# Attention with an MLP behind it: the first chunk's softmax sums in 64x32 tiles, and one load moved to another queue

## The chip, the cores and the metric

One core of a Trainium2 chip runs the whole program. The time is device microseconds (us) from start to end of one execution; the kernel before took 416.88 us (median of 3 runs, 416.04 to 417.06). The profile is of one more execution, whose span is 417.9 us. The engines are TensorE (PE in the profile; its weight loads are PEld), VectorE (DVE), ScalarE (ACT), GpSimd (POOL), and SyncE (SP), which only issues transfers.

## The reference, cut to what matters

```python
q, k, v: (8 batches, 12 heads, 448 positions, 64)      # float32
q_n, k_n = q / rms(q) * g_q, k / rms(k) * g_k           # rms over the 64
scores = q_n @ k_n.T / 8
attn = exp(scores - max) / (sum(exp(scores - max)) + 1e-9)
x = (attn @ v), heads side by side                       # (3584, 768)
h = x @ w_in                                             # (3584, 2048)
g = h + sin(alpha * h) ** 2 / alpha
out = g @ w_out                                          # (3584, 768)
```

The kernel takes exp without subtracting the maximum, since normalised queries and keys keep the scores small. What matters here is the denominator: for each head and each query the sum of exp over 448 keys, and then the product of `attn @ v` with its reciprocal.

## The kernel before, in words

**Chunks.** The 12 heads of a batch are worked on in three chunks of four heads. In a chunk, a head has an index `pp` (which half of the 128 SBUF partitions its keys lie on) and an index `hi` (which half of a tile's columns). Chunk number `ci` is 3 times the batch plus 0, 1 or 2. `load_qk(ci)` fetches q and k of a chunk, `load_v(b, c)` fetches v. The first two chunks of the program have been special: the loads of their k were issued by ScalarE (`load_qk(0, nc.scalar)`, `load_qk(1, nc.scalar)`), all others by SyncE.

**Plans.** The order of work on every engine is written out by hand. The strings `STAGE_0` (batch 0), `STAGE_1` (batch 1) and `STAGE_N` (batches 2 to 7) list tokens, and every engine executes its instructions strictly in the order in which the tokens issue them:

- `q`, `u`, `r`, `g`, `k`, `t` with a chunk: square (GpSimd, L283), reduce (VectorE, L292), reciprocal root (ScalarE, L301 and L302), fold in the gains (GpSimd, L288), scale (GpSimd, L311), transpose by a transfer that SyncE issues (L321). A second digit is q (0) or k (1). Chunks 3 to 5 in a plan are those of the next batch.
- `S`: one score tile, four matmuls of 64x64 with 448 columns (L358), and its exp on ScalarE (L361).
- `o`, `v`: for the batch's first chunk, the matmuls that sum exp over the keys with a matrix of ones ("ones 0") and those with v ("values 0"), seven key tiles each (L406). `x`, `y`, `z`: the same for the second and third chunks together, in tiles of 64x32 already. A digit says how many key tiles.
- `f` or a number: steps of the second product of the batch before, used as filler between score tiles: eight matmuls of 64x64 with 384 columns each (L528).
- `V`, `l`: loads of v (issued by GpSimd) and of q and k (issued by SyncE).

After the plan comes `first_product` (96 matmuls of 128x128 with 448 columns, L449, with the sine on ScalarE at L427), beside which the tokens of a second table run at the given step (`h_plan`). So a stage is: 56 filler steps, 21 score tiles, `o`, `v`, `x`, `y`, `z`, then the first product. After the last batch the second product runs alone (L509).

**PSUM.** There are four pairs of banks. The digit string of a stage says which pair each new PSUM tile takes; it has to have been given back by its last user.

**The step that is touched.** `attend(b, "ones 0")`: for each of seven key tiles, four matmuls of 64x64, one for each (`hi`, `pp`); the weights are ones, the moving side is exp with 448 queries, and the output strip `o` is 64 partitions, so that the same sum stands on all 64 partitions on which the head's 64 output features will stand. Then ScalarE takes Ln and Exp(-x) of the whole [128, 2, 448] tile (L412, L413), which is the reciprocal `rec`, and VectorE multiplies the values by it (L421).

Of the kernel before, what the change touches and what calls it, by code (L numbers as in the profile page):

```python
# [17 lines left out]
try:  # L18
# [8 lines left out]
ACT = mybir.ActivationFunctionType  # L27
# [22 lines left out]
)  # L50
STAGE_N = (
    (
# [3 lines left out]
    ),  # L56
    "01232302102020301301320321310130210231023",
    {-1: 'l6 u51 V12', 1: 'k41', 2: 't4 l7', 3: 'g5'},
)
LAST = "0123012"  # L60

# [7 lines left out]
def kernel(  # L69
# [23 lines left out]
    nc = tc.nc  # L93
    B, H, S, D = q.shape
# [8 lines left out]
    NJ = S // REST  # L103
    assert P == 2 * REST == 2 * D
    NC = NP // 2
# [28 lines left out]
    def bank_pair(name, dtype=F32):  # L134
        slot = int(upcoming.popleft())
        free_at.remove(slot)
        ps = psum.tile([P, 2, 2048 // mybir.dt.size(dtype)], dtype, tag=f"ps{slot}", name=name)
        slot_of[id(ps)] = slot
        return ps

    def give_back(ps):
        free_at.append(slot_of.pop(id(ps)))
# [3 lines left out]
    def strip(c, pp, hi):  # L146

        s = 2 * hi + (pp if c == 1 else 1 - pp)
        return slice(s * 32, s * 32 + 32)

    def load_qk(ci, k_queue=nc.sync):

        b, dp = ci // NC, ci % NC
        qk[ci] = inp.tile([P, 2, 2 * NJ, D], F32, tag="qk", name="qk")
        for which, src, queue in ((0, q, nc.sync), (1, k, k_queue)):
            heads = src[b].rearrange("(dp hi pp) (p j) d -> dp pp p hi (j d)", hi=2, pp=2, j=NJ)[dp]
            rows = qk[ci][:, which].rearrange("p (hi j) d -> p hi (j d)", hi=2)
            if ci == 0:
                continue
            if dp < 2:  # L160
                queue.dma_start(out=rows, in_=heads.rearrange("pp p hi x -> (pp p) hi x"))
            else:
                for pp in range(2):
                    queue.dma_start(out=rows[pp * 64:pp * 64 + 64], in_=heads[1 - pp])
        if ci == 0:
            for hi in range(2):
                for which, src, queue in ((0, q, nc.sync), (1, k, k_queue)):
                    heads = src[b].rearrange("(dp hi pp) (p j) d -> dp hi pp p (j d)", hi=2, pp=2, j=NJ)[dp, hi]
                    rows = qk[ci][:, which].rearrange("p (hi j) d -> p hi (j d)", hi=2)
                    queue.dma_start(out=rows[:, hi], in_=heads.rearrange("pp p x -> (pp p) x"))  # L170
                if hi == 0:
                    load_g()
# [17 lines left out]
    def load_g():  # L190
        for i, (src, queue) in enumerate(((g_q, nc.sync), (g_k, nc.scalar))):
            queue.dma_start(out=g_rows[:, i], in_=src.rearrange("(a d) -> a d", a=1))

    load_qk(0, nc.scalar)
    load_qk(1, nc.scalar)
    load_qk(2)
    nc.gpsimd.dma_start(out=small, in_=moe_alpha.rearrange("(mt p) -> mt p", p=P))
    nc.scalar.preload_act_table_set(EXP_LN)
# [2 lines left out]
    ones = const.tile([P, D], BF16)  # L201
# [58 lines left out]
    qkT, expT, xT = {}, {}, {}  # L260
# [125 lines left out]
    def attend(b, what, tiles=range(NJ)):  # L386

        kind, both = what.split()  # L390
        both = both == "1"
        if tiles[0] == 0:
            avs[what] = bank_pair("av")
        av = avs[what]
        pre = presums.get(b) if what == "ones 0" else None
        last = 1 if pre else NJ - 1
        for j in tiles:
            for hi in range(2):
                for c in ((1, 2) if both else (0,)):
                    for pp in range(2):  # L400
                        r = slice(pp * 64, pp * 64 + 64)
                        o, k = (strip(c, pp, hi), c - 1) if both else (slice(hi * 64, hi * 64 + 64), pp)
                        d = slice(kind == "high", D, 2) if both and kind != "ones" else slice(D // 2 if both else D)
                        w = ones[r, d] if kind == "ones" else vb[b][r, 2 * c + hi, j, d]
                        x = pre.parts[j] if pre else expT[b * NC + c, j]
                        nc.tensor.matmul(av[o, k, :S], w, x[r, hi, :], start=(j == 0), stop=(j == last))  # L406
        if tiles[-1] < last:
            return
        if kind == "ones":
            rec = recs[both] = pre.t if pre else rpool.tile([P, 2, S], F32, tag="rec", name="rec")  # L410
            for k in ((0, 1), (1, 2)) if both and b == 0 else ((0, 2),):
                nc.scalar.activation(rec[:, slice(*k)], av[:, slice(*k), :S], ACT.Ln)  # L412
                nc.scalar.activation(rec[:, slice(*k)], rec[:, slice(*k)], ACT.Exp, scale=-1.0)  # L413
            give_back(avs.pop(what))
        else:
            if b not in xT:
                xT[b] = xpool.tile([P, KT, S], BF16, tag="xT", name="xT")
            first = 0 if not both else 2 if kind == "low" else 3
            for k in (slice(0, 1), slice(1, 2)) if both and b == 0 else (slice(0, 2),):
                kts = slice(first + k.start * (1 + both), first + (k.stop - 1) * (1 + both) + 1, 1 + both)  # L420
                nc.vector.tensor_mul(xT[b][:, kts, :], av[:, k, :S], recs[both][:, k])  # L421
            give_back(avs.pop(what))
# [185 lines left out]
    for b in range(B):  # L608
        plan, slots, h_plan = (STAGE_0, STAGE_1, STAGE_N)[min(b, 2)]
        if b:  # L610
            nc.scalar.preload_act_table_set(EXP_LN)
            fillers.extendleft(reversed(second_product(b - 1)))
        tiles = deque((b * NC + c, j) for c in range(NC) for j in range(NJ))
        upcoming.extend(slots)
        done = {what: 0 for what in STEPS}
        for x in tokens_of(plan):
            if x in "Ff":
                fill(x == "f")
            elif x[0] == "S":
                scores(*tiles.popleft(), int(x[1:] or 0))  # L620
            elif x[0] in STEPS:
                n = int(x[1:] or 1)
                attend(b, STEPS[x[0]], range(done[x[0]], done[x[0]] + n))
                done[x[0]] += n
            else:
                step(b, x)
        first_product(b, {i: [lambda t=t: step(b, t) for t in tasks.split()] for i, tasks in h_plan.items()})
        assert not upcoming and not tiles
# [32 lines left out]
```

## Time and profile before

| what | value |
|---|---|
| time, median of 3 | 416.88 us |
| span of the profile | 417.9 us |
| busy: PE, ACT, POOL, DVE | 95%, 76%, 68%, 54% |
| granted TensorE clock | full speed (0.998) |
| first product of batch 0 waits for its last weights until | 41.79 us |
| from one first product's start to the next, batches 2 to 7 | 47.3 us |
| last first product ends, second product alone begins | about 393 us |
| transfers | 54.5 MB, 130 GB/s over the span |

A stage's time is read from the start of one block of L449 matmuls to the next. The busy share of PE over the span is held down by the first 42 us (loads and the first batch's normalisation) and by a few waits in the stage of batch 1; how full the later stages are is shown further down. Every row's count and mean duration come from the groups of instructions, and the spacing of matmuls from the timeline of PE.

### The profile page before, as it was taken

What the parts mean: (1) busy time and instruction counts of PE and PEld (TensorE: products, weight loads), DVE (VectorE), ACT (ScalarE), POOL (GpSimd) and SP (SyncE); (2) the same over time, 40 slices, a digit from 0 to 9 for tenths busy, and PEclk for the clock granted to TensorE, in tenths of its full rate; (3) what the DMA queues carried; (4) which work ended last, traced back from release to release, by engine and by line L of the source; (5) the groups of instructions that cost most, each with busy time, mean ns of one, the idle gap of its engine ahead of it and who ended that gap; (6) DMA issues with size and microseconds to landing.
All of it is one profiled execution on the core that took longest, in us unless ns stands there. A gap on an engine that the chain in (4) does not pass through costs nothing.

```text
span 417.9 us, 14897 instructions
## 1 busy us (share of the span) xinstructions
PE 397.1 (95%) x6598; PEld 238.2 (57%) x6601; DVE 227.1 (54%) x339; ACT 317.4 (76%) x467; POOL 285.3 (68%) x270
## 2 busy tenths in 40 slices
PE   2797999889999999999999999999999999999996
PEld 2243558645666557655666456655576556665563
DVE  5786475426674565564575466655565464335511
ACT  4897789748889679877889688987889688886600
POOL 4999889966786879597796688597795784003300
PEclk9999999999999999999999999999999999999999
DMA  8999999798085744847374744736385521620022
GB/s 244 212 220 255 167 218 156 168 284 105 3 164 131 168 139 83 175 92 156 101 175 119 174 134 80 176 81 164 104 131 158 93 46 27 96 61 0 2 75 75
DMA packets 66788, 54.51 MB, mean 130 GB/s; under 512 B 38164, under 2 KB 62500, under 8 KB 66724
## 3 DMA queue, kind: packets, MB, share of 16 engines
q1 hardware_dynamic: 53250, 40.06, 37.8%
q0 software_dynamic: 12512, 11.81, 19.7%
q10 hardware_dynamic: 962, 1.70, 1.1%
q8 instruction: 51, 0.84, 0.8%
q14 instruction: 13, 0.11, 0.1%
HBM read 45.62 MB, written 11.01 MB: 136 GB/s over the span
## 4 chain that ended last, share of the span: by engine, by line
PE 86%; DMA 6%; POOL 4%; issue 2%; DVE 1%; ACTq 0%; SPq 0%; ACT 0%; DVEq 0%; POOLq 0%
PE hps L449 34%; PE ops L528 29%; PE av L406 11%; PE sc L358 6%; PE ops L509 5%; DMA w_in<-in_moe_w_in_dram 3%; DMA qk<-in_k_dram 2%; POOL sq L283 1%; DMA out_dram<-osb 1%; POOL qk L288 1%; POOL vb L182 0%; POOL vb L185 0%; SPq L499 0%; POOL w_in L244 0%; DVE osb L534 0%
## 5 line engine op out<-in xcount | busy, mean ns | idle before, releaser
L361 ACT ACTIVATE expT<-sc 128x896 bf16<-128x896 f32 x168 | 144.9, 914 | 16.9 <-PE sc L358 16.0
L449 PE MATMUL hps<-xT,w_in 128*128 128x448 bf16 x768 | 146.8, 353 | 2.1 <-DMA w_in<-in_moe_w_in_dram 2.1
L528 PE MATMUL ops<-w_out_sb,g_sb 64*64 64x384 bf16 x3072 | 145.6, 323 | 0.2 <-ACT expT L361 0.2
L435 DVE SCALAR_TENSOR_TENSOR g_sb<-s,inv_alpha_sb,hps 128x448 bf16<-128x448 f32 x128 | 80.8, 677 | 67.3 <-POOL s L430 66.9
L449 PEld LDWEIGHTS <-w_in 128*128 128x128 bf16 x768 | 74.4, 98 | 74.0 <-issue 3.0
L528 PEld LDWEIGHTS <-g_sb 64*64 64x64 bf16 x3072 | 91.3, 107 | 38.0 <-issue 2.7
L430 POOL TENSOR_TENSOR s<-s 128x448 f32<-128x448 f32 x64 | 59.5, 932 | 74.7 <-ACT s L427 50.2
L427 ACT ACTIVATE s<-hps,alpha_sb 128x448 f32<-128x448 f32 x128 | 74.4, 626 | 43.2 <-PE hps L449 40.4
L283 POOL TENSOR_TENSOR sq<-qk 128x896 f32<-128x896 f32 x44 | 73.3, 1682 | 26.1 <-DMA qk<-in_k_dram 21.1
L311 POOL TENSOR_TENSOR qkn<-qk,inv 128x448 bf16<-128x448 f32 x80 | 72.7, 938 | 2.5 <-ACT inv L302 2.0
L358 PE MATMUL sc<-qkT 64*64 64x448 bf16 x672 | 58.3, 356 | 3.6 <-DVE qkT L343 2.1
L534 DVE COPY osb<-ops 128x384 f32<-128x384 f32 x48 | 26.7, 557 | 51.3 <-PE ops L528 46.1
L288 POOL TENSOR_TENSOR qk<-qk,gg 128x896 f32<-128x896 f32 (+1 forms) x25 | 50.3, 2016 | 1.2 <-ACT g_sb L280 1.1
L292 DVE TENSOR_REDUCE ms<-sq 128x14 f32<-128x896 f32 x44 | 46.7, 1078 | 6.4 <-POOL sq L283 6.3
L421 DVE TENSOR_TENSOR xT<-av,rec 128x896 bf16<-128x896 f32 (+1 forms) x26 | 25.6, 1015 | 37.2 <-ACT rec L413 30.7
L406 PE MATMUL av<-expT,vb 64*32 64x448 bf16 (+1 forms) x1120 | 37.9, 350 | 2.7 <-issue 2.0
L432 ACT ACTIVATE s<-s 128x448 f32<-128x448 f32 x64 | 36.9, 577 | 3.0 <-DVE g_sb L435 0.2
L358 PEld LDWEIGHTS <-qkT 64*64 64x64 bf16 x672 | 20.7, 107 | 17.3 <-issue 7.9
L406 PEld LDWEIGHTS <-vb 64*32 64x32 bf16 (+1 forms) x1120 | 19.5, 95 | 16.7 <-issue 6.8
L535 DVE TENSOR_TENSOR osb<-osb,ops 128x384 f32<-128x384 f32 x48 | 26.6, 554 | 1.7
L406 PE MATMUL av<-expT,ones 64*32 64x448 bf16 (+1 forms) x672 | 24.5, 349 | 0.0
L509 PE MATMUL ops<-w_out_sb,g_sb 128*128 128x384 bf16 x128 | 21.0, 326 | 0.0
(46 smaller groups left out, 173.5 us busy)
## 6 DMA issues: line engine op xcount, KB each, us to landing
out_dram<-osb SPq DMA_DIRECT2D x39, 192.0 KB, 3.7
qk<-in_q_dram SPq DMA_DIRECT2D x15, 448.0 KB, 5.5
qk<-in_k_dram SPq DMA_DIRECT2D x14, 448.0 KB, 6.3
qk<-in_q_dram SPq DMA_DIRECT2D x18, 224.0 KB, 4.3
qk<-in_k_dram SPq DMA_DIRECT2D x16, 224.0 KB, 4.7
vb<-in_v_dram POOLq DMA_DIRECT2D x16, 224.0 KB, 4.4
w_out_sb<-in_moe_w_out_dram POOLq DMA_DIRECT2D x4, 768.0 KB, 7.7
out_dram<-osb SPq DMA_DIRECT2D x26, 96.0 KB, 3.4
```

The source lines that it names most:

```text
L283: nc.gpsimd.tensor_mul(st.sq[w], qk[ci][:, w], qk[ci][:, w])
L288: nc.gpsimd.tensor_mul(x, x, gg.to_broadcast([P, len(heads) * NJ, D]))
L292: nc.vector.reduce_sum(st.ms[:, w, rows], st.sq[w][:, rows], axis=AX.X)
L311: eng.tensor_mul(n[:, :, hi, :], x[:, hi], inv[:, hi].unsqueeze(2).to_broadcast([P, NJ, D]))
L358: nc.tensor.matmul(sc[pp * 64:pp * 64 + 64, hi, :S], qkt[r, 1, j * REST:(j + 1) * REST], qkt[r, 0, :], start=True, stop=True)
L361: nc.scalar.activation(expT[c, j], sc[:, :, :S], ACT.Exp, scale=SCALE)
L406: nc.tensor.matmul(av[o, k, :S], w, x[r, hi, :], start=(j == 0), stop=(j == last))
L427: nc.scalar.activation(s1, hps, ACT.Sin, scale=alpha_sb[:, m, :])
L430: nc.gpsimd.tensor_mul(s2, s1, s1)
L435: nc.vector.scalar_tensor_tensor(g_sb[:, m, (b % 2) * S:(b % 2 + 1) * S], s2, inv_alpha_sb[:, m, :], hps, op0=ALU.mult, op1=ALU.add)
L449: nc.tensor.matmul(ps[:, m % 2, :S], w_in_sb[m * 2 // MT][:, kt, m % (MT // 2) * P:(m % (MT // 2) + 1) * P], x[:, kt, :], start=(kt == ORD ...
L528: nc.tensor.matmul(st["ps"][os, r, :HALF], g_sb[rs, m, c0 + o * 64:c0 + o * 64 + 64], w_out_sb[rs, m, half * HALF:(half + 1) * HALF], star ...
```

## The change

The sums of the first chunk, for all batches but the first, no longer use four 64x64 tiles but eight of 64x32: the 448 queries are split in two halves (`qh`), and each half's sum goes to its own strip of 32 partitions. This uses 32 columns of ones where 64 held the same value, and each matmul streams 224 columns where it streamed 448; there are twice as many. A head's 64 partitions then hold, in their two strips of 32, two different halves of the queries, both in columns 0 to 223. ScalarE takes Ln of that half width, writes Exp(-x) once to columns 224 to 447 and once in place, and four transfers from SBUF to SBUF, issued by SyncE, bring each strip's reciprocals to the partner strip. After that `rec` is as it was.

The plan of batches 2 to 7 is replaced: `o7` stands earlier, among score tiles and fillers, and `v` follows in three pieces after seven more score tiles. The order of GpSimd's work, of the loads and of the PSUM pairs changes with it. `STAGE_1` stays as it is. The loads of k for the second chunk of the program go to SyncE's queue.

```diff
 STAGE_N = (
     (
-        "1 r2 q31 q30 f 2 S V10 f 3 V11 f f k20 2 S 3 S 2 k21 S u31 q40 1 t2 1 g3 1 S 1 f u30 S 2 f S f S "
-        "r3 q41 f f 1 l5 1 f S 4 u40 S S 5 S S u41 o7 v7 S S 5 S 2 q51 f S 2 S q50 k31 k30 2 S g4 1 u50 S "
-        "2 r4 t3 1 S z3 x7 k40 y7 z1 z2 z1 "
+        "q40 f V11 5 f 1 f S f 1 S g4 2 f r2 f S u40 1 f S 1 f S 2 S k21 2 S k20 t2 q30 2 f 1 S q31 f f 1 "
+        "l5 f S o7 1 u30 2 q41 V12 u31 1 S 2 S 2 S 3 r3 1 u41 S 1 V10 g3 1 q51 S S 3 S v2 v4 S v1 k30 2 S "
+        "1 S 1 S 3 S k31 r4 1 x7 y7 t3 z7 q50 "
     ),
-    "01232302102020301301320321310130210231023",
-    {-1: 'l6 u51 V12', 1: 'k41', 2: 't4 l7', 3: 'g5'},
+    "01232313130132332302312310213212301230123",
+    {-1: 'k40', 0: 'g5 u51 l6', 2: 'k41 t4', 8: 'u50 l7'},
 )
-    load_qk(1, nc.scalar)
+    load_qk(1)
+        halved = what == "ones 0" and b > 0
         for j in tiles:
+            if halved:
+                for hi in range(2):
+                    for qh in range(2):
+                        for pp in range(2):
+                            r, o = slice(pp * 64, pp * 64 + 64), slice((2 * hi + qh) * 32, (2 * hi + qh) * 32 + 32)
+                            nc.tensor.matmul(av[o, pp, :S // 2], ones[r, :D // 2], expT[b * NC, j][r, hi, qh * S // 2:(qh + 1) * S // 2],
+                                             start=(j == 0), stop=(j == NJ - 1))
+                continue
...
+            if halved:
+                cols = [slice(0, S // 2), slice(S // 2, S)]
+                nc.scalar.activation(rec[:, :, cols[0]], av[:, :, cols[0]], ACT.Ln)
+                nc.scalar.activation(rec[:, :, cols[1]], rec[:, :, cols[0]], ACT.Exp, scale=-1.0)
+                nc.scalar.activation(rec[:, :, cols[0]], rec[:, :, cols[0]], ACT.Exp, scale=-1.0)
+                for hi in range(2):
+                    for qh in range(2):
+                        src, dst = (slice((2 * hi + x) * 32, (2 * hi + x) * 32 + 32) for x in (qh, 1 - qh))
+                        nc.sync.dma_start(out=rec[dst, :, cols[qh]], in_=rec[src, :, cols[qh]])
```

More of the change, by code (lines that the diff above doesn't have):

```diff
@@ L410, in attend @@
             rec = recs[both] = pre.t if pre else rpool.tile([P, 2, S], F32, tag="rec", name="rec")
-            for k in ((0, 1), (1, 2)) if both and b == 0 else ((0, 2),):
+            if halved:
[7 more added lines that the diff above has]
+                        nc.sync.dma_start(out=rec[dst, :, cols[qh]], in_=rec[src, :, cols[qh]])
+            for k in () if halved else ((0, 1), (1, 2)) if both and b == 0 else ((0, 2),):
                 nc.scalar.activation(rec[:, slice(*k)], av[:, slice(*k), :S], ACT.Ln)
```

## The prediction, made before the changed kernel was run

> **What bounds the kernel now.** I read three views in this order. First the chain of waits that ended last, to see which engine carries the time:
>
> ```profile
> PE 86%; DMA 6%; POOL 4%; issue 2%; DVE 1%; ACTq 0%; SPq 0%; ACT 0%; DVEq 0%; POOLq 0%
> PE hps L449 34%; PE ops L528 29%; PE av L406 11%; PE sc L358 6%; PE ops L509 5%; DMA w_in<-in_moe_w_in_dram 3%; DMA qk<-in_k_dram 2%; POOL sq L283 1%; DMA out_dram<-osb 1%; POOL qk L288 1%; POOL vb L182 0%; POOL vb L185 0%; SPq L499 0%; POOL w_in L244 0%; DVE osb L534 0%
> ```
>
> TensorE's own work is the chain, and av L406, which holds the edited matmuls, has 11% of it. Second, busy times by stretches, cut at the starts of the first products, to see whether a stage has any idle PE time to lose or to win:
>
> ```profile
> 90.20:137.50 47.30, 47.30 (x853) 28.82 (x854) 27.76 (x41) 37.97 (x57) 32.16 (x28) 1.00 0.58 115
> 137.50:184.80 47.30, 47.30 (x855) 28.82 (x854) 27.08 (x40) 39.06 (x58) 37.34 (x34) 1.00 0.58 136
> 280.00:327.30 47.30, 47.25 (x855) 28.83 (x852) 27.09 (x40) 39.05 (x58) 37.07 (x34) 1.00 0.58 134
> ```
>
> The columns are length, then PE, PEld, DVE, ACT and POOL busy, then clock, DMA share and GB/s. PE is busy for 47.30 of 47.30 us: these stages are as long as TensorE's work, so each us of PE work that goes is a us of time, until ACT (39) or POOL (37) becomes the bound. Third, PE's timeline in one stage, for the spacing of the matmuls:
>
> ```profile
> 218.49 1.49 PE L406 MATMUL av<-expT,ones 64*64 64x448 bf16 x28
> 219.82 1.49 PE L406 MATMUL av<-expT,vb 64*64 64x448 bf16 x28
> ...
> 227.67 0.36 PE L358 MATMUL sc<-qkT 64*64 64x448 bf16 x4
> 227.96 0.76 PE L406 MATMUL av<-expT,vb 64*32 64x448 bf16 x24
> 228.53 1.51 PE L406 MATMUL av<-expT,ones 64*32 64x448 bf16 x56
> 229.86 1.89 PE L406 MATMUL av<-expT,vb 64*32 64x448 bf16 x72
> ```
>
> The first column is the start. The 28 edited matmuls take 219.82 - 218.49 = 1.33 us to the next group's start: seven waves of four tiles, 0.19 each. At 64x32, 56 matmuls take 229.86 - 228.53 = 1.33 us: seven waves of eight, also 0.19. The tiles run side by side and the columns streamed set the time. From the last 64x64 wave to the first 64x32 wave it is 0.29 where a wave is 0.19: a change of tile shape costs 0.10.
>
> [...] The trace is already at 1.33/56 = 23.8 ns with tiles side by side, [...] but nothing in it shows a lasting rate faster than that, and the change asks for 12 ns. [...] The smallest stores in the trace, 96 KB, land 3.4 us after issue on SyncE and 2.4 on ScalarE[...].
>
> **The matmuls, batches 2 to 7.** Length against columns: L449 (448 columns) runs 96 matmuls in 18.27 us of the chain, 0.190 each; L509 (384 columns) 128 in 20.82, 0.163 each. That is 0.027 for 64 columns, so 224 columns fewer make a wave of 0.190 - 3.5 x 0.027 = 0.096. Seven waves of eight tiles: 0.67 us. Removed: 1.33. Gross gain 0.66 a stage.
>
> The new plan puts `o7` between a score tile and a filler step, both 64x64; before it stood among 64x64 work and needed no change of shape. So two are added. Entering costs 0.10. Leaving is in the stage of batch 1:
>
> ```profile
> 83.13 0.38 PE L406 MATMUL av<-expT,vb 64*32 64x448 bf16 x8 [0.43 <-DVE osb L535]
> 83.45 0.38 PE L358 MATMUL sc<-qkT 64*64 64x448 bf16 x4
> 83.76 0.38 PE L406 MATMUL av<-expT,vb 64*32 64x448 bf16 x8
> ```
>
> 0.32 and 0.31 between starts, so 0.13 for leaving. Together 0.23; net 0.66 - 0.23 = 0.43 a stage. `v`, now in three pieces, is 64x64 among 64x64 work, and `x y z` enters and leaves its shape once as before. Six stages: **2.6 us**.
>
> **The same in batch 1.** There the old plan gives `o2` and `o5` apart: four changes of shape, 0.66 - 0.46 = 0.20. I count it as nothing. Behind it PE waits for a chain that its matmuls don't set: SyncE issues two transposes from 71.66 to 75.09 as soon as GpSimd has scaled chunk 2, then six stores, whose landing at 81.81 frees the output buffer that VectorE needs at 81.93. The four new transfers come after the fourth of those stores, so the two tiles waited for are not delayed, but chunk 5's loads and the later stores are, by four issues of about 0.6 = 2.4 us. GpSimd's square of chunk 5 then ends near 89.5 in place of 87 and its work up to the snake near 93.5; the first sine comes 4.4 us into the first product (237.0 against 232.6 in a later stage), here at 94.6. Hidden, by 1 us.
>
> **ScalarE.** Ln and Exp of 896 columns go (0.92 + 0.95); Ln at 448 (0.53) and two Exps at 448 (0.58 each) come: 1.69 for 1.87. ACT is busy 39 of 47, so this is worth nothing.
>
> **The four transfers.** Each moves 32 x 2 x 224 x 4 bytes = 57 KB. Issue: 0.36 to 0.70 us on SyncE's rows; I take 0.6, so 2.4 us a stage on an engine that issues for some 18 of 47 us (six transposes at 1.33, eight loads at 0.65, eight stores at 0.6). Landing: 2.4 to 4.3 us (the smallest store, a 224 KB load); I take 3. Dating the new plan on PE's clock, with 0.325 for a filler step and 0.19 for a score tile: `o7` runs at 11.8 to 12.7 us of the stage, ScalarE is done by about 14.5, SyncE has issued `t2` and `l5` by about 15.2, the transfers by 17.6, and they land at 20.6 (20.0 to 21.9). The multiplication by `rec` follows `v1`, which ends at 21.1 by the same count. So they are just hidden; VectorE may sit up to 0.8 us on them. Behind it on VectorE wait the copies of output tiles out of PSUM, and for those PE. With four bank pairs and ScalarE's exps ahead of the score tiles I expect such a wait to be absorbed.
>
> **The rest of the new plan.** GpSimd starts a stage with `q40`, which needs `l7`, issued late in the stage before. `k41` ends some 2 us later than before, so `l7` is issued at about 247 where it was 244.8 in the stage of 203 to 251; q of it landed 3.6 to 3.8 us after issue in those windows, thus at 251. GpSimd's last snake square ends 1.8 us into the new stage, later than that: no wait. From there q 1.64, V 0.74, g 2.07 and `k21 k20` 3.62 end at 9.9 us; `t2` lands by 14.6. Chunk 2's first score tile, the 15th, comes at 18.2: 3.6 us of slack. The sums per engine are those of before.
>
> **The head.** The k of the second chunk is issued by SyncE behind its q: at about 2.5 in place of 2.16. GpSimd's gate waits for that k until 10.44 now, ScalarE's squares until 10.40. On one queue q and k of chunk 1 come ahead of chunk 2's loads, which SyncE issues from 4.40, so the k may land earlier by up to 2 us. But the chain goes on to the weights at 41.79, with the DMA engines 80 to 90% busy in every slice up to there: an earlier gate mostly reorders the same bytes. At most the 2.1 us that the first product waits for w_in; I take 0.3.
>
> **Sum.** 416.88 - 2.6 - 0.3 = 414.0.
>
> **Rivals.** (a) Rate of instructions: [...] 419 in all. For it: [...] a rate never seen here. Against: waves at 23.8 ns already, and PEld is busy only 28.8 of 47.3. Chance 0.12. (b) SyncE's queue: transfers late, VectorE held, then PE. If they land 2 us later than I say, or the stores behind them do, a stage loses 0.3 to 1.3 of what it won: 415.5 to 421, middle 418. For it: only 0.5 us of slack[...]. Against: SyncE idle more than half the stage. Chance 0.16. (c) The head does move by 1 to 2 us: 412.5. For it: the chain passes through that k. Against: busy DMA. Chance 0.14. The forecast: 0.58, spread 413.4 to 414.8.
>
> **How the numbers follow.** Faster (below 415.6): 0.58 + 0.14 + 0.02 of (b) = 0.74. Same: 0.08, from (b). Slower: 0.12 + 0.06 = 0.18. The range runs from 412.2, within (c), to 418.4, within (b), and leaves out (a), the worse half of (b) and the lower part of (c), about 0.2.
>
> **What would show it.** In the timeline after, the 56 matmuls of the sums should span 0.67 us plus 0.23 of edges, stages should measure 46.87, and PE should have no idle time in them. [...] PE idle released by VectorE, with VectorE released by a transfer of `rec`, proves (b). A first product of batch 0 that resumes well before 41.8 proves (c). Stages of 47.3 or more would make the forecast wrong.

## The result, and the profile after

The changed kernel takes 439.91 us (median; 438.48 to 442.74), the kernel before 416.46 in the same session: ratio 1.0575, interval 1.0517 to 1.0633. It is slower by 5.7%. The forecast was 414.0, and the time lies far above the range too. Below, medians take all runs of a kernel, and ratios leave out runs that are more than 1.5% above its fastest.

The chain of waits that ended last, of the kernel after:

```profile
PE 73%; DMA 14%; ACT 5%; SPq 3%; DVE 3%; issue 1%; DVEq 0%; POOL 0%; POOLq 0%
PE hps L467 33%; PE ops L546 21%; PE av L415 8%; DMA rec<-rec 7%; PE ops L527 5%; PE sc L358 4%; DMA qk<-in_k_dram 4%; ACT expT L361 3%; SPq L428 2%; DMA w_in<-in_moe_w_in_dram 2%; DVE xT L439 2%; PE av L404 1%; DVE ms L292 1%; SPq L517 1%; ACT rec L423 1%
```

TensorE had 86% of it before, now 73%. A row that did not exist is fourth: the landing of the new transfers, 7% of 441 us, with their issue on SyncE (L428) at 2% and VectorE's multiplication (L439) at 2%. So the path that sets the end leaves TensorE, and it leaves it for the transfers.

Busy times by stretches, of the kernel after, cut at the starts of the first products (columns as in the prediction):

```profile
196.21:247.28 51.07, 48.73 (x881) 29.28 (x882) 27.11 (x40) 39.09 (x59) 36.84 (x33) 0.97 0.59 130
350.79:397.69 46.90, 46.90 (x881) 28.63 (x882) 22.95 (x36) 37.95 (x55) 14.80 (x15) 1.00 0.26 66
```

Two things are to be seen. The last stage, that of batch 7, is 46.90 us long and full: the forecast for every stage was 46.87. This batch has no next one, so no q, k or v is loaded while its transfers run. The other five are 51.1 to 52.0 us long, have 2.3 to 3.3 us of idle PE time (51.07 - 48.73 = 2.34 in the one shown), and their clock is 0.97 where it was 1.00. What they have and the last has not is loads.

PE's timeline of the kernel after, in the stage that starts at 196.21:

```profile
226.01 0.36 PE L358 MATMUL sc<-qkT 64*64 64x448 bf16 x4
226.30 0.86 PE L404 MATMUL av<-expT,ones 64*32 64x224 bf16 x56
227.10 1.49 PE L546 MATMUL ops<-w_out_sb,g_sb 64*64 64x384 bf16 x32
...
236.84 0.50 PE L546 MATMUL ops<-w_out_sb,g_sb 64*64 64x384 bf16 x8
239.68 0.38 PE L358 MATMUL sc<-qkT 64*64 64x448 bf16 x4 [2.35 <-DVE xT L439]
```

The 56 sums take 227.10 - 226.30 = 0.80 us with the edge behind them, and their entry 0.29 where a wave is 0.19: what the prediction worked out (0.67, and edges of 0.10 and 0.13). Ten microseconds later PE stands for 2.35 us, released by VectorE's multiplication. VectorE's and SyncE's timelines of the kernel after, of the same stage:

```profile
238.54 1.09 DVE L439 TENSOR_TENSOR xT<-av,rec 128x896 bf16<-128x896 f32 x1 [3.38 <-DMA rec<-rec]
```

```profile
224.51 3.41 SPq L321 DMA_TRANSPOSE qkT<-qkn  x2
227.97 1.40 SPq L164 DMA_DIRECT2D qk<-in_q_dram  x2
229.41 1.26 SPq L164 DMA_DIRECT2D qk<-in_k_dram  x2
230.77 3.01 SPq L428 DMA_DIRECT2D rec<-rec  x4
```

SyncE issues two transposes, then chunk 5's loads (`l5`, four of 224 KB), and only then the four transfers; VectorE starts on what they bring at 238.54. The last `v` matmul ends at about 235.7, so VectorE is about 2.9 us late, and the pair of banks that `v` holds goes back that much later. At 239.68 a score tile needs that pair. ScalarE had `rec` ready early: its last Exp starts at 228.42.

PE's idle time is not the whole loss. Busy times of the kernel after, in three stretches of 3.41 us around the wait:

```profile
237.27:240.69 3.42, 1.07 (x29) 0.87 (x28) 1.09 (x1) 1.58 (x3) 3.42 (x4) 1.00 0.46 160
240.69:244.10 3.41, 3.41 (x71) 1.61 (x68) 1.11 (x2) 1.69 (x4) 3.41 (x4) 0.50 0.02 5
244.10:247.51 3.41, 3.41 (x138) 1.76 (x123) 0.87 (x1) 2.75 (x3) 1.47 (x2) 1.00 0.52 126
```

The sixth number after the length, counts in brackets left out, is the granted clock: 1.00, then 0.50 for 3.41 us, then 1.00 again. At 0.50 TensorE was half as fast: in the window from 42.71 to 46.13, also at 0.50, the matmuls of L467 started 0.373 us apart, behind it 0.189. So 3.41 us at half speed cost 1.71. Idle 2.35 plus 1.71 is 4.06, of the 51.07 - 46.90 = 4.17 that this stage loses.

The clock records of the twelve traces say more. In each of them the clock changes only at multiples of 3.413 us, counted from the trace's first record. Cut into such windows, 1374 of them at full speed, the traces show one limit: all 28 windows in which PE stood idle for 2.11 us or more were followed by a window at half speed, and none of the other 1346, with 1.90 us or less, was (idle times by PE's records, whose ends are modelled). Both ends of the limit stand in the trace of after: 2.11 in the window from 83.67 to 87.09, 1.90 in that from 435.25 to 438.66. What counts is thus how much of a wait falls into one window. In the kernel before, PE waited 2.14 us for weights (39.65 to 41.79), but a boundary cut that wait in two, and the clock stayed at 1.00:

```profile
37.23:40.65 3.42, 2.42 (x20) 1.06 (x12) 3.00 (x5) 2.23 (x3) 3.42 (x3) 1.00 1.10 256
40.65:44.06 3.41, 2.27 (x12) 1.19 (x13) 1.26 (x2) 0.17 (x1) 3.21 (x2) 1.00 1.13 212
```

### The profile page after: what moved, and what is told of

Same layout as the page of the kernel before. It is cut to its first block, busy times and chain, and to the rows that moved or that the text cites. A ratio compares the mean times of both kernels' runs of the same rounds, so it can differ in the third digit from the quotient of the medians.

```text
span 441.0 us, 15366 instructions
## 1 busy us (share of the span) xinstructions
PE 406.5 (92%) x6794; PEld 239.3 (54%) x6797; DVE 227.7 (52%) x339; ACT 317.5 (72%) x474; POOL 285.6 (65%) x270
## 4 chain that ended last, share of the span: by engine, by line
PE 73%; DMA 14%; ACT 5%; SPq 3%; DVE 3%; issue 1%; DVEq 0%; POOL 0%; POOLq 0%
PE hps L467 33%; PE ops L546 21%; PE av L415 8%; DMA rec<-rec 7%; PE ops L527 5%; PE sc L358 4%; DMA qk<-in_k_dram 4%; ACT expT L361 3%; SPq L428 2%; DMA w_in<-in_moe_w_in_dram 2%; DVE xT L439 2%; PE av L404 1%; DVE ms L292 1%; SPq L517 1%; ACT rec L423 1%
## 5 line engine op out<-in xcount | busy, mean ns | idle before, releaser
L546 PE MATMUL ops<-w_out_sb,g_sb 64*64 64x384 bf16 x3072 | 154.0, 330 | 0.2 <-ACT expT L361 0.2
L467 PE MATMUL hps<-xT,w_in 128*128 128x448 bf16 x768 | 148.5, 355 | 2.7 <-DMA w_in<-in_moe_w_in_dram 2.7
L467 PEld LDWEIGHTS <-w_in 128*128 128x128 bf16 x768 | 74.8, 98 | 75.9 <-issue 4.6
L546 PEld LDWEIGHTS <-g_sb 64*64 64x64 bf16 x3072 | 92.8, 109 | 39.8 <-issue 4.5
L358 PE MATMUL sc<-qkT 64*64 64x448 bf16 x672 | 62.6, 364 | 16.6 <-DVE xT L439 15.8
L292 DVE TENSOR_REDUCE ms<-sq 128x14 f32<-128x896 f32 x44 | 47.3, 1081 | 14.7 <-POOL sq L283 14.7
L439 DVE TENSOR_TENSOR xT<-av,rec 128x896 bf16<-128x896 f32 (+1 forms) x26 | 25.7, 1016 | 46.7 <-ACT rec L431 24.4
L358 PEld LDWEIGHTS <-qkT 64*64 64x64 bf16 x672 | 22.3, 108 | 32.1 <-issue 23.3
L415 PEld LDWEIGHTS <-vb 64*32 64x32 bf16 (+1 forms) x1120 | 19.6, 97 | 14.0 <-issue 2.8
L415 PE MATMUL av<-expT,ones 64*32 64x448 bf16 (+1 forms) x476 | 17.3, 423 | 0.0
```

Of the source, the lines that this page charges most:

```text
L292: nc.vector.reduce_sum(st.ms[:, w, rows], st.sq[w][:, rows], axis=AX.X)
L358: nc.tensor.matmul(sc[pp * 64:pp * 64 + 64, hi, :S], qkt[r, 1, j * REST:(j + 1) * REST], qkt[r, 0, :], start=True, stop=True)
L467: nc.tensor.matmul(ps[:, m % 2, :S], w_in_sb[m * 2 // MT][:, kt, m % (MT // 2) * P:(m % (MT // 2) + 1) * P], x[:, kt, :], start=(kt == ORD ...
L546: nc.tensor.matmul(st["ps"][os, r, :HALF], g_sb[rs, m, c0 + o * 64:c0 + o * 64 + 64], w_out_sb[rs, m, half * HALF:(half + 1) * HALF], star ...
```

## The experiments

Times are medians; the ratio is to the kernel before on the same chip (416.46 beside after, 417.08 to 417.30 beside the others). Diffs are against the kernel after unless said otherwise. In the plan of batches 2 to 7, `l5` is chunk 5's loads on SyncE, `V12` and `V10` loads of v on GpSimd.

| run | time | ratio (interval) | landing of the transfers, median |
|---|---|---|---|
| after | 439.91 | 1.0575 (1.0517 to 1.0633) | 5.8 |
| e1, ScalarE issues the transfers | 443.90 | 1.0647 (1.0578 to 1.0716) | 6.5 |
| e2, `l5` behind the transfers | 417.82 | 1.0017 (0.9993 to 1.0041) | 4.2 |
| e3, no transfers | 415.54 | 0.9950 (0.9928 to 0.9972) | none |
| e4, new plan, 64x64 sums | 420.62 | 1.0069 (1.0048 to 1.0090) | none |
| e5, before with the k load alone | 417.40 | 1.0000 (0.9980 to 1.0019) | none |
| e6, e2 and v's loads behind too | 421.71 | 1.0092 (1.0067 to 1.0117) | 2.9 |
| e7, e6 from batch 2 on | 420.06 | 1.0062 (1.0028 to 1.0095) | 2.4 |
| e8, e2 with ScalarE issuing | 442.99 | 1.0624 (1.0586 to 1.0662) | 6.1 |
| e9, e2 from batch 2 on | 417.70 | 0.9997 (0.9972 to 1.0022) | 3.5 |
| e10, old plan, halved from batch 2 on | 449.13 | 1.0760 (1.0728 to 1.0793) | 2.1 |

**e1: another engine issues.**

```diff
-    nc.sync.dma_start(out=rec[dst, :, cols[qh]], in_=rec[src, :, cols[qh]])
+    nc.scalar.dma_start(out=rec[dst, :, cols[qh]], in_=rec[src, :, cols[qh]])
```

> The changed kernel, with the four transfers of the reciprocals issued by ScalarE instead of SyncE; nothing else. Theory Q (the transfers wait in SyncE's queue behind the 0.9 MB of chunk 5's loads issued just ahead of them): they land 2 to 3 us after issue where the changed kernel had a median of 5.8, VectorE's multiplication by rec no longer waits, stages of batches 2 to 6 go from 51.6 to about 47.0, time 415 to 419. Theory C (the 16 DMA engines are shared, and any traffic of that moment, loads of v too, slows the transfers whatever queue they are on): landing stays at 5 us or more, stages 50 or more, time 430 to 438.

443.90 us. The row of DMA issues of this kernel:

```profile
rec<-rec ACTq DMA_DIRECT2D x28, 56.0 KB, 6.5
```

From a queue of their own, issued at once after Exp, the transfers take 6.5 us to land, not less: theory C's landing, and theory Q falls. The DMA packets in the traces show how. In after, in the stage shown above, the packets of `rec` begin at 234.98, 4.2 us after the first issue, when those of `l5` on the same queue (229.46 to 236.11) are nearly through. Here, in the stage shown below, they begin at 126.03, 2.2 us after the first issue, but of their 320 packets 56 move up to 127.03, another 76 up to 130.00 and the other 188 up to 132.41, while the packets of `l5` and of v's loads run up to 131.85 and 132.26. So leaving SyncE's queue does not free the transfers from the loads: they start earlier and are drawn out. From 125 to 132 the packets of SyncE's, GpSimd's and ScalarE's queues took 49.5%, 46.6% and 10.9% of the span of the 16 DMA engines, in sum 107%. The time, longer than either theory had, was lost in another place, seen in the timelines of ScalarE and PE:

```profile
123.83 3.20 ACTq L428 DMA_DIRECT2D rec<-rec  x4
127.07 2.54 ACT L361 ACTIVATE expT<-sc 128x896 bf16<-128x896 f32 x3 [3.27 <-issue]
```

```profile
128.04 0.38 PE L358 MATMUL sc<-qkT 64*64 64x448 bf16 x4 [2.97 <-ACT expT L361]
```

ScalarE computes nothing in the 3.2 us in which it issues; the next exp is 3.27 us late and PE waits 2.97 for it. Half speed follows here too (the stage's clock record shows it from 128.82 to 132.23). Even the last batch, which has no loads, is 51.26 us long.

**e2: the loads behind the transfers.**

```diff
-        "l5 f S o7 1 u30 2 q41 V12 ...
+        "f S o7 1 u30 2 l5 q41 V12 ...
```

> The changed kernel, with the token l5 (the loads of chunk 5) moved in the plan of batches 2 to 7 to behind o7, u30 and two filler steps, so that SyncE issues the transfers ahead of these loads. Theory Q: the transfers land 2 to 3 us after issue, no wait for rec; the loads come 2.5 us later, which GpSimd's square of chunk 5 may feel by 2 to 3 us; stages 47 to 48.5, time 416 to 424. Theory C: the loads, though issued behind, and the loads of v share the engines with them: landing 4 to 6 us, stages 49.5 to 51, time 428 to 437.

417.82 us: 22 us less than after, and no difference from before. That is theory Q's time, with theory C's landing (2.0 to 4.9 us, median 4.2). SyncE's timeline of this kernel:

```profile
218.45 3.16 SPq L428 DMA_DIRECT2D rec<-rec  x4
221.66 1.35 SPq L164 DMA_DIRECT2D qk<-in_q_dram  x2
```

The edit takes away two delays at once. In batches 2 to 6, counted from the end of the first product, the last of the four transfers is issued at 17.08 on average (after: 19.00), and the multiplication starts at 21.55 (after: 24.61), where 21.36 is the earliest that `v1` allows. So 1.92 of the 3.06 us come from SyncE's issuing, and the rest from landing. By estimate neither alone would have done: issued at 19.00 and landing 4.2 later, `rec` would be there at 23.2, and in e1, with issues from 14.6 to 17.7, it is there at about 23. What still moves beside the transfers are the loads of v (in the stage shown their packets run from 219.90 to 224.55, those of `rec` from 220.12 to 224.70). The stages are now 47.09 to 47.27 long in batches 3 to 6 (48.41 in batch 2, 46.90 in batch 7), none of these stages has half speed, and VectorE's waits for `rec` sum up to 4.3 us where they were 21.2.

**e3: no transfers.**

```diff
-                for hi in range(2):
-                    for qh in range(2):
-                        src, dst = (slice((2 * hi + x) * 32, (2 * hi + x) * 32 + 32) for x in (qh, 1 - qh))
-                        nc.sync.dma_start(out=rec[dst, :, cols[qh]], in_=rec[src, :, cols[qh]])
```

> The changed kernel without the four transfers: each strip keeps only its own half of the queries right, the rest of the tile is left with the other half's values, so the output is not the reference's. If the transfers are the whole loss: stages 46.9, no wait for rec, time 413.5 to 415. Theory P (the new plan by itself makes waits, the bank order or the loads): stages stay at 48 or more and time above 420.

415.54 us, 0.5% under before. This kernel leaves half of each `rec` tile with the values of the other half of the queries, so its output is not the reference's; all its other work is that of after. It shows what the change can bring with transfers that cost nothing; the 24.4 us between it and after are theirs. Two stages of this kernel, by stretches:

```profile
134.14:182.14 48.00, 47.26 (x896) 29.31 (x880) 27.52 (x40) 39.38 (x59) 37.04 (x34) 1.00 0.61 133
276.67:323.57 46.90, 46.90 (x896) 28.70 (x880) 27.11 (x40) 38.87 (x59) 36.47 (x34) 1.00 0.60 137
```

Three of six stages are 46.90, two of them with their loads. The other three (47.54, 48.00, 47.63) have small waits of PE (0.23, 0.74, 0.23) that end in nothing that the profile shows:

```profile
181.68 0.72 PE L415 MATMUL av<-expT,vb 64*32 64x448 bf16 x17 [0.74 <-issue]
```

**e4: the plan without the halving.**

```diff
-        halved = what == "ones 0" and b > 0
+        halved = False
```

> The new plan and the k load on SyncE's queue, with the sums in 64x64 tiles as before the change (no transfers). Transfers to blame: stages 47.3, time 416 to 417.5, the same as before. Theory P: stages of 49 or more, time above 425.

420.62 us, 0.69% above before, 3 us more than expected if the transfers alone were to blame. Two of its stages:

```profile
134.30:181.64 47.34, 47.34 (x868) 30.13 (x852) 27.22 (x40) 38.91 (x58) 35.21 (x34) 1.00 0.61 136
276.70:326.20 49.50, 48.03 (x868) 30.06 (x852) 27.68 (x40) 39.70 (x58) 39.43 (x36) 1.00 0.55 130
```

The undisturbed one is as long as before (47.3), so halving is worth 47.34 - 46.90 = 0.44 a stage, against 0.43 worked out. The 49.50 has a wait "issue" of 1.26 us ahead of L546. The medians of e4 and e3 differ by 5.1 us where six times 0.44 make 2.6; the other 2.5 are not explained.

**e5: the k load alone**, on the kernel before.

```diff
-    load_qk(1, nc.scalar)
+    load_qk(1)
```

> The kernel before with only the second chunk's k moved to SyncE's queue. If the head is bound by the total of transfers, as the prediction had it: 416.5 to 417.5, no difference that can be measured. Rival: q and k of the second chunk, alone on one queue ahead of the third chunk's, land 1.5 to 2 us earlier and the whole head moves: 414.5 to 415.5.

417.40 against 417.30: no difference, as expected. That the bytes bound the head is the prediction's reason; no run tests it.

**e6: v's loads behind the transfers too.**

```diff
-        "l5 f S o7 1 u30 2 q41 V12 u31 ... 1 S 1 V10 g3 ... v2 v4 S v1 k30 ...
+        "f S o7 1 u30 2 l5 q41 u31 ... 1 S 1 g3 ... v2 v4 S v1 V12 V10 k30 ...
```

> As e2_load_after, and the loads of v (V12, V10) of batches 2 to 7 also moved, to behind v1. Theory C (the transfers wait for whatever the DMA engines have been given before them, on any queue): nothing is ahead of the transfers now, they land 2.0 to 2.6 us after issue in batches 2 to 7, where e2 had a median of 4.2; VectorE never waits for rec there; stages 46.9, time 415 to 417. If landing stays near 4, the v loads are not what is left, and the transposes or the stores are.

The landing falls to 2.9 us, and VectorE waits for `rec` in batch 1 only (1.6 us): with no loads ahead of them and v's no longer beside them, the transfers are in time. But the time is 421.71 where 415 to 417 was expected: the loads are now too late for those who need them. The waits of this kernel (total us, times, longest):

```profile
POOL sq L283 <- DMA qk<-in_k_dram: 27.9, 4, 8.4
PE hps L467 <- DVE g_sb L453: 3.4, 4, 1.3
```

GpSimd stands on its squares, its part of the sine step in the first product comes late, VectorE's `g_sb` behind it, and PE waits for that. Clearing the way for one transfer is paid by another.

**e7: the same, halved from batch 2 on.**

```diff
-        halved = what == "ones 0" and b > 0
+        halved = what == "ones 0" and b > 1
```

> As e6_v_after_too, with the sums in 64x32 tiles from batch 2 on only: batch 1 keeps the 64x64 sums and has no transfers. If the transfers of batch 1 delay the output stores behind them on SyncE's queue, as in the changed kernel, where PE waited 2.2 us for VectorE there: 1 to 2.5 us less than e6, 413.5 to 415.5. If batch 1 waits for the stores anyway: the same as e6 within 0.5.

420.06, by the ratios 0.3% less than e6, with overlapping intervals, and not the 413.5 to 415.5 expected: the halving in batch 1 is no gain that can be seen and may be a small loss.

**e8: e2's order, with ScalarE issuing.**

> As e2_load_after, with the four transfers issued by ScalarE. Separates the two losses of e1_act_queue. If there the issue itself was the loss (3.2 us on ScalarE between two exps, then PE idle 3 us for want of a bank): still slow, stages 49 to 52, 430 to 442, although the transfers land in 4 us or less. If ScalarE's issues were only slow because the engines were loaded: issues of 0.6 each, stages 47 to 48.5, 417 to 424.

442.99 us, landing 6.1 and not the 4 or less expected, so the run does not separate the two losses as it was meant to. The order was lost: SyncE, no longer held by the transfers, issued `l5` at 173.63, ahead of ScalarE's transfers at 174.74. So a token's place in the plan orders two transfers only if one engine issues both. ScalarE's loss is that of e1, with an exp 3.33 us late behind the issues:

```profile
174.74 3.26 ACTq L428 DMA_DIRECT2D rec<-rec  x4
```

**e9: e2, halved from batch 2 on.**

> As e2_load_after (chunk 5's loads behind the transfers), with the sums in 64x32 tiles from batch 2 on only. In e2 batch 1 waited for VectorE and its late rec by about 1 us; without transfers in batch 1 that goes, and 0.2 us of the gain of batch 1 with it: 416 to 417.5, at or a little under the time before. If the new plan itself costs the 3 us that e4_plan_alone showed and e2 only balances it, not below 416.5.

417.70 (413.06 to 419.97), ratio 0.9997: the lowest ratio with transfers, no different from e2's within the noise, and equal to before. No run that computes the whole is faster than the kernel before.

**e10: before's plan, halved from batch 2 on** (the k load as in after).

> The 64x32 sums with their transfers from batch 2 on, in the old plan of batches 2 to 7, where o7 stands directly ahead of v7 and the loads of chunk 5 are 3 us older. The matmuls need no further change of shape costs than in the new plan. The transfers are issued when v7 is nearly done and land 2.5 us or more after, so VectorE's multiplication is 4 us late or more. If what PE waits for is the PSUM bank that v holds, as in the changed kernel, stages of 48 to 51 and 420 to 438; if the old bank order spares that bank long enough, stages of 46.9 to 47.3 and 414 to 417.

449.13 us, the slowest and above the 420 to 438 expected, though the transfers land fastest, in 2.1 us (in the stage shown, the packets of `l5` end at 232.69 and those of `rec` begin at 232.85). SyncE's and VectorE's timelines of this kernel:

```profile
231.52 2.63 SPq L428 DMA_DIRECT2D rec<-rec  x4
```

```profile
235.68 1.09 DVE L439 TENSOR_TENSOR xT<-av,rec 128x896 bf16<-128x896 f32 x1 [5.61 <-DMA rec<-rec]
```

In the old plan `v7` follows `o7` at once and ends at 230.60, so the values are ready 5.1 us before Ln, two Exps, four issues and the landing are through. PE then waits 3.06 us for the banks of `v`, and runs at half clock behind it (0.50 from 236.80 to 238.00). So the new plan was needed: it sets the end of `o7` 8.5 us ahead of the end of `v`. It did not set it far enough ahead of a landing behind loads.

## Why the prediction was wrong, point by point

**The matmuls: right.** 0.80 us for the 56 with the edge behind them, 46.90 for an undisturbed stage against 46.87, 0.44 a stage by e3 and e4 against 0.43. Rival (a), by which the matmuls can't start much faster than the 23.8 ns each of the kernel before, was the author's assumption and is refuted: the trace has the 56 starts between 226.30 and 226.91, 11 ns each, in waves about 0.096 us apart with 2 to 4 ns between the tiles of a wave.

**The transfers: here it failed,** in two terms and one inference.

- The issuing. The prediction had `t2` and `l5` issued "by about 15.2", the transfers by 17.6. In batches 2 to 6 the first transfer is issued at 16.77 on average and the last is through at 19.60. The transposes took 3.41 us in the stage shown where 2.66 was counted, and a transfer costs about 0.7, not 0.6. Together 2.0 late.
- The landing. "2.4 to 4.3 us (the smallest store, a 224 KB load); I take 3." Measured after the last issue: 24.6 - 19.6 = 5.0, or 5.8 (median) from each issue. The size does not set it: the same 56 KB land in 2.0 in the stage of batch 7, which has no loads. `l5` and v's loads, 0.92 and 0.46 MB, are given to the DMA engines from 227.97 to 231.1; their packets move from 229.46 to 237.69, and those of `rec` from 234.98 to 237.85, with the end of them. Another 2.0 late, so 24.6 in place of 20.6.
- "I expect such a wait to be absorbed." With 2.9 us of lateness only 0.5 was: PE was idle 2.35 us in the stage shown, up to 3.27 in another. And the wait then cost 1.71 more by the clock, a term that no step had.

The sum of a stage: 46.90 with idle 2.35 to 3.27 and half clock 1.7 is, within 0.3, the 51.1 to 52.0 measured in five stages. This is rival (b) in its mechanism, both of whose signs came (PE released by VectorE, VectorE by a transfer of `rec`), and it was given 0.16 and up to 1.3 us a stage, less than a third of the real loss.

The trace of before had the hint, in its groups of DMA issues:

```profile
vb<-in_v_dram POOLq DMA_DIRECT2D x16, 224.0 KB, 4.4
...
vb<-in_v_dram POOLq DMA_DIRECT2D x16, 112.0 KB, 5.4
```

Half the size landed a microsecond later. A landing had to be read from what else is under way at that moment, not from the nearest size.

**Batch 1: "I count it as nothing".** It loses in the same way as the others, by a wait that the prediction left out: it asked what the transfers delay on SyncE's queue, and not when `rec` arrives. They are issued from 80.26 to 82.94, behind four stores; the last `v` matmul of the chunk ends at 83.77. PE and VectorE of the kernel after, and the stretch behind the wait:

```profile
87.77 0.59 PE L358 MATMUL sc<-qkT 64*64 64x448 bf16 x4 [2.18 <-DVE xT L439]
```

```profile
86.63 1.09 DVE L439 TENSOR_TENSOR xT<-av,rec 128x896 bf16<-128x896 f32 x1 [2.10 <-DMA rec<-rec]
```

```profile
87.09:90.50 3.41, 2.73 (x52) 1.15 (x59) 0.63 (x1) 0.92 (x1) 1.52 (x3) 0.50 1.04 246
```

From the first product's resumption to the next one's start it is 51.0 us against 48.4, with PE idle for about as long in both (3.5 and 3.6): what was added is half speed. Another window at half speed lies earlier (42.71 to 46.13), in the first product, which takes 1.7 us longer behind its wait of 2.70 for weights. That one is not put down to the change: the wait is there in the kernel before too (2.14), cut in two by a boundary. e7 against e6 and e9 against e2 test the halving there, and neither shows a difference beyond the noise.

**The rest of the plan: "no wait".** Half right. Undisturbed stages are full with it, but e4 is 0.69% above before. What ends PE's waits "issue" is open. Busy DMA engines are not common to them: the DMA share was 0.02 and 0.07 in the longest of e3 and e4, and 1.10 in one of 1.60 us in batch 1 of the kernel before.

**The head: not contradicted.** e5 shows no difference; its interval, 0.8 us to either side, is too wide to tell 0.3 from nothing. GpSimd's gate moved from 10.44 to 9.19 in e5's trace (10.11 in after), and e5's time did not follow. Rival (c), 1 to 2 us, falls. Its sign, an earlier resumption, can't be read from one trace: e5's has no wait for weights at all, and in the kernels that share this head the first product of batch 0 ends anywhere between 55.2 and 59.9.

**The order of sizes.** Plan and load about +3 (e4 against before), halving -5 (e3 against e4), transfers +24 (after against e3): of these, 22 stem from the place behind the loads (after against e2) and 2.3 remain with that order (e2 against e3), nearly what the halving was predicted to bring.

## What to carry to other kernels

Before a transfer is put between two engines on the critical path, date it by the bytes that all engines have given to DMA just before, and by what its issuing engine still has to issue; its own size says little (here 56 KB landed in 2.0 us with no loads, in 4.9 to 7.0 behind 1.38 MB of them). Order a short, urgent transfer ahead of bulk loads on the same issuing engine (22 us here, e2), and see who then gets the loads late. And price a wait of a busy TensorE above its idle time: behind 2.35 us of it came 3.41 us at half clock, and in these traces the limit lay between 1.90 and 2.11 us of idle time within one window of 3.41.

## What the runs showed of the hardware that was not expected

- A 56 KB transfer within SBUF landed 2.0 us after issue in a stage without loads, 4.9 to 7.0 in batches 2 to 6 of after, behind 1.38 MB of loads, and 6.5 (median) from ScalarE's queue beside the same loads.
- Four issues took ScalarE 3.20 us in the stage shown of e1 and 3.26 in that of e8, in which it computed nothing; on SyncE they took 2.62 us in the last batch of after, without loads, and 3.01 in the stage shown.
- In the twelve traces the clock of TensorE changed on a grid of 3.413 us. A window with 2.11 us or more of idle PE (28 of 28) was followed by one at 0.50, a window with 1.90 or less (1346 of 1346) was not. Of the windows at half speed, 28 with 0.69 us or less of idle PE were followed by full speed (all 7 of after among them, with 0.00 to 0.69), and 4 with 0.89 or more by half speed again.
- Eight 64x32 tiles of 224 columns ran in waves of 0.096 us (after), half of the 0.19 of those of 448 columns.
